# Seven-product Q/K projection: two products and the loads around them reordered, results stored over three products

## The chip, the cores and the metric

One core of a Trainium2 chip runs the whole kernel. The metric is the device time of one execution in microseconds (us); the median of a few runs is what counts.

## The reference

```python
x = A_x                                  # 1 x 2048 x 1024, float32
xn = _layernorm(x)
q, k, v = split_heads(xn @ wqkv)         # 32 heads of 32 columns
o = softmax(q k^T / sqrt(32)) v          # per head, over all 2048 positions
s = merge_heads(o) @ wo
g = silu(mish(xn @ w1 + b1) @ w2)        # inner width 3584
out = x + s * g
```

All inputs and the output are float32.

## The kernel before

Every large matrix product is done in float32r with both operands split: `high` is the value copied into float32r by ScalarE (`copy`), `low` is what is left (`low`, a subtraction on VectorE or GpSimd). A product is then three matmuls, high·high, high·low and low·high (`THREE`).

The kernel runs in stages. First x is normalised, transposed and split into eight resident tiles `xc[c][g]` (chunk c of 512 tokens, half g of the 1024 columns), while V is computed. Then comes the Q/K stage, which the change concerns. Last comes a long stage of attention and the two dense layers, whose order a planner writes out (`Plan`), and a short tail for the output product.

**The Q/K stage.** There are 16 rounds q. A round takes 128 columns of the Q part of `wqkv` (`raw` tile r0) and 128 of the K part (r1), each 1024 x 128, and two chunks of tokens: chunks 2 and 3 for q below 8, chunks 0 and 1 from q = 8. It makes the 2 x 2 blocks of the result with seven products in place of eight. The products of a round are numbered i = 0 to 6 and named `A11, S2, A12, S3, S1, A22, S4`; a product (q, i) is 12 matmuls of 128 x 512. Its two operands are
- a piece of W (`piece`): a quarter of r0 or r1, or a sum S1 to S4 of quarters that GpSimd makes (`w_sum`, line 551) one round ahead; ScalarE and VectorE split it (`wq` tiles, two of two pieces each);
- a half chunk of x, or a sum of such half chunks, in `X[0]` (q below 8) or `X[1]` (from 8). The sums T0 to T3 for the second half of the rounds lie in DRAM (`ts`); they are loaded 128 x 512 at a time into `traw` buffers by `t_load`, and split into x tiles whose last reader in the first half is past: T1 into xc[2][0], T2 into xc[2][1], T0 into xc[3][0], T3 into xc[1][0]. The odd one of each pair of quarters has its low part made by GpSimd. One plain x half chunk, `X[1][6]`, is read back from `xs` in four loads into xc[1][1] (`B_COUNT`).

Products of a round add up in three PSUM banks, x, y and z. What is finished is added to an earlier result by VectorE (`plus`, line 775), split by `out_` into a `qst` tile and stored to `qs` or `ks` by a DMA of ScalarE's queue.

**What sets the order.** The order is written by hand in one loop over `SEQ`. For product number n the loop emits the 12 matmuls; then, at even n, the pieces n + 2 and n + 3 with the loads and sums that hang on them; then what `later.at(t, ...)` had put off to this product (`later.tick`); from (11, 2) on two score matmuls of head 0 with a maximum on VectorE each (`s_mm`, lines 695 and 699); then `after()`, the copies and additions for the result; and last the loads counted from product (7, 0) by `since`. Each engine and queue then runs its own list in that order and waits where an operand or a buffer is not ready. SyncE's queue carries all loads.

`EARLY` moves a few products of rounds 7 and 8 forward, so that the x tiles come free for T0 to T3 before they are needed. `q_load` loads the two W tiles of a round (512 KB each) into the buffers of the round two before.

Of the kernel before, what the change touches and what calls it, by code (L numbers as in the profile page):

```python
# [9 lines left out]
F32 = mybir.dt.float32  # L10
# [8 lines left out]
P = 128  # L19
# [211 lines left out]
def body(ctx: ExitStack, tc: tile.TileContext, x, wqkv, wo, w1, b1, w2, out):  # L231
    nc = tc.nc
# [6 lines left out]
    def pool(stack, name, bufs, side="left", **kw):  # L239
        return stack.enter_context(tc.tile_pool(name=name, bufs=bufs, side=side, reuse_waits="tile", **kw))  # L240

    def psum(stack, name, bufs):
        return stack.enter_context(tc.tile_pool(name=name, bufs=bufs, space=PSUM, reuse_waits="tile"))
# [43 lines left out]
    def copy(out_, in_, scale=1.0):  # L287
        nc.scalar.activation(out_, in_, AF.Copy, scale=scale)  # L288

    def move(out_, in_, eng=None):  # L290

        (eng or nc.sync).dma_start(out_.bitcast(F32), in_.bitcast(F32))

    def low(eng, out_, in_, high):

        eng.tensor_tensor(out_, in_, high.bitcast(F32), ALU.subtract)  # L296
# [6 lines left out]
    later = Later()  # L303
# [231 lines left out]
    A11, S2, A12, S3, S1, A22, S4 = range(7)  # L535
    NQ = 2 * KT
    raws, sums, pieces = {}, {}, {}

    def q_load(q, tiles):
        raws[q] = tiles  # L540
        for half in range(2):
            col = half * D + q % KT * P
            nc.sync.dma_start(tiles[half], wqkv[:, col:col + P].rearrange("(k p) f -> p k f", p=P))

    def w_sum(eng, q, which, out_):
        (r0, r1), done = raws[q], sums.setdefault(q, {})
        done[which] = out_
        a, b, how = {S1: lambda: (r1[:, :HK], r1[:, HK:], ALU.add), S2: lambda: (done[S1], r0[:, :HK], ALU.subtract),
                     S3: lambda: (r0[:, :HK], r1[:, :HK], ALU.subtract),
                     S4: lambda: (r0[:, HK:], done[S2], ALU.subtract)}[which]()  # L550
        eng.tensor_tensor(out_, a, b, how)

    EARLY = {(6, 2): [(7, 0)], (6, 3): [(7, 2)], (6, 4): [(7, 1)], (7, 4): [(8, 0)]}
    MOVED = [x for v in EARLY.values() for x in v]
    SEQ = [x for q in range(NQ) for i in range(7) if (q, i) not in MOVED for x in [(q, i)] + EARLY.get((q, i), [])]
    held = {w: big.tile([P, HK, P], F32, tag=f"ws{w}", name=f"ws{w}") for w in (S1, S3, S4)}

    def piece(n, eng):
        q, i = SEQ[n]
        if n % 2 == 0:  # L560
            pieces["tile"] = w1_tile(f"wq{n // 2}")
        w = pieces[n] = pieces["tile"][:, :, n % 2 * HK:n % 2 * HK + HK]
        if i == A22:
            src = raws[q][1][:, HK:] if q else held[S3]
        else:
            src = raws[q][0][:, :HK] if i == A11 else raws[q][0][:, HK:] if i == A12 else sums[q][i]
        copy(w[:, 0], src, scale=-1.0 if i == A22 else 1.0)
        if i == A22:
            nc.vector.scalar_tensor_tensor(w[:, 1], src, -1.0, w[:, 0].bitcast(F32), op0=ALU.mult, op1=ALU.subtract)
        else:  # L570
            low(eng, w[:, 1], src, w[:, 0])
# [49 lines left out]
    halves = [(p, k, half) for p in (1, 0) for k in range(HK) for half in range(2)]  # L621
# [30 lines left out]
    ring = [ra.tile([P, KT, P], F32, name=f"raw{i}") for i in range(4)]  # L652
    qb = ExitStack()
    sp = pool(qb, "sp", 1)
    psq = psum(qb, "psq", 2)
    qst, kst = [], []

# [81 lines left out]
            move(dst[:, :, k], src[:, :, k])  # L739

    def t_load(i, k):
        raw, dst = sp.tile([P, 512], F32, tag="traw", name=f"t{i}_{k}", bufs=4), X[1][T_UNIT[i]]
        nc.sync.dma_start(raw, ts[i][:, k])

        def split():
            copy(dst[:, 0, k], raw)
            low(nc.gpsimd if k % 2 else nc.vector, dst[:, 1, k], raw, dst[:, 0, k])

        later.at(2, split)

    X = ([xc[2][0], xc[3][0], xc[2][1], xc[1][0], xc[1][1], xr, xc[3][1]],
         [xc[0][0], xc[2][0], xc[0][1], xc[2][1], xc[3][0], xc[1][0], xc[1][1]])
    BANK = ("x", "y", "x", "y", "z", "y", "z")
    T_UNIT = (4, 1, 3, 5)
    T_ORDER = [(i, k) for i in (1, 2, 0, 3) for k in range(HK)]
    T_COUNT = (2, 1, 1) * 4
    B_COUNT = {9: (0,), 10: (1,), 11: (2,), 12: (3,)}
    spare = []

    def ring_of(q):  # L760
        if q < KT + 2:
            return ring[q % 2 * 2:q % 2 * 2 + 2]
        if not spare:
            spare.append(big.tile([P, 4, KT, P], F32, tag="xc3_1", name="spare"))
        return [spare[0][:, q % 2 * 2 + half] for half in range(2)]

    def out_(q, half, chunk_, src):
        st = sp.tile([P, 2, 512], F32R, tag="qst", name=f"qst{q}_{half}_{chunk_}", bufs=4)
        copy(st[:, 0], src)
        low(nc.vector, st[:, 1], src, st[:, 0])  # L770
        dst = (qs, ks)[half][q % KT].rearrange("h p n -> p h n")[:, :, chunk_ * 512:(chunk_ + 1) * 512]
        later.at(2, lambda: move(dst, st, nc.scalar))

    def plus(out_, a, b):
        nc.vector.tensor_tensor(out_, a, b, ALU.add)
# [39 lines left out]
    for n, (q, i) in enumerate(SEQ):  # L815
        after = product(n)
        for m in (n + 2, n + 3) if n >= 2 and n % 2 == 0 else ():
            if m >= 7 * NQ:
                continue
            piece(m, nc.vector if q < 11 or m % 2 else nc.gpsimd)  # L820
            q_, i_ = SEQ[m]
            if i_ == A22:
                if q_ == 9:
                    ra_.close()
                    early = pool(att0, "early", 1, side="right")
                    stacks(early, 0)
                    stacks(early, 1)
                    hl_ = early.tile([P, P], F32R, name="hl")
                    nc.gpsimd.memset(hl_.bitcast(F32), 0.0)
                    nc.gpsimd.memset(early.tile([P, 32], F32, name="pad2"), 0.0)  # L830
                if q_ + 2 < NQ and q_ != 7:
                    q_load(q_ + 2, ring_of(q_ + 2))
            if q_ + 1 < NQ:
                for which in {S1: (S1, S2), A22: (S3,), S4: (S4,)}.get(i_, ()):
                    w_sum(nc.gpsimd, q_ + 1, which, s_tile(which))
        later.tick()
        if (q, i) >= (11, 2):
            for qt, kc in [x for _, x in zip(range(2), first_s)]:
                s_mm(0, qt, kc)
        after()  # L840
        since = n - SEQ.index((KT - 1, 0))
        if 0 <= since < len(T_COUNT):
            for _ in range(T_COUNT[since]):
                t_load(*T_ORDER.pop(0))
        if since == 11:
            q_load(9, ring_of(9))
        for k in B_COUNT.get(since, ()):
            move(X[1][6][:, :, k], xs[1][:, :, HK + k])
        if i == 0 and q == 10:
            load_head(0)  # L850
        if i == 3 and q == 14:
            load_head(1)
        if i == 5 and q == NQ - 1:
            load_w1(0)
# [638 lines left out]
    for c in range(NC):  # L1493
        for s in range(4):
            t = 4 * c + s
            if t + 4 < NT:
                start(t + 4)
            for dh in range(2):
                k = 2 * s + dh
# [45 lines left out]
```

## Time and profile before

| | |
|---|---|
| median of 3 runs | 3377.38 us (3376.79 to 3378.0) |
| the profiled execution | 3378.28 us |
| its span | 3376.5 us |
| TensorE busy | 3346.0 us, 99% of the span |
| VectorE, ScalarE, GpSimd busy | 74%, 61%, 75% |
| the Q/K stage | 202.16 us to 536.38 us of the span |

The span runs from the first instruction to the last; 1.78 us of the profiled execution lie outside it. Matmuls are pipelined: a product of 12 shows 2.88 us, while the next one starts 2.72 us after it. So the start-to-start distance is what tells whether TensorE was held up.

### The profile page before, as it was taken

To read this page: it belongs to the slowest core of one execution; us is meant where nothing else is said; L and a number is where in the kernel's file an instruction comes from. 1 tells how busy PE (TensorE), PEld (TensorE's weight loads), DVE (VectorE), ACT (ScalarE), POOL (GpSimd) and SP (SyncE) were. 2 spreads that over 40 slices of the span, in tenths; PEclk is the share of its full clock that TensorE was granted. 3 is DMA by queue.
4 is the path that set the end of the run, shared out by engine and by line. 5 is a ranking of instruction groups with operands and counts; after the bars stand their busy time and mean duration, and the time that the engine had idled before them with its cause. 6 is when DMAs were issued, how large, how long until landed. Compare 5 with 4: busy or idle time off the path is not lost.

```text
span 3376.5 us, 45751 instructions
## 1 busy us (share of the span) xinstructions
PE 3346.0 (99%) x16867; PEld 2455.0 (73%) x16867; DVE 2511.8 (74%) x3984; ACT 2055.8 (61%) x3314; POOL 2525.0 (75%) x751
## 2 busy tenths in 40 slices
PE   8999999999999999999999999999999999999999
PEld 7888777777777677777667767677667777767787
DVE  6665678888777777887888778788777888886542
ACT  5233425677667666667666766667667766667621
POOL 2322445999999977889888988888888898889800
PEclk9999999999999999999999999999999999999999
DMA  7864745455555643434344434333344433433482
GB/s 243 298 208 158 244 156 164 135 175 169 169 173 173 218 132 112 123 102 118 118 120 147 144 101 125 90 111 113 113 150 127 127 98 112 125 118 106 136 301 87
DMA packets 291460, 501.56 MB, mean 149 GB/s; under 512 B 88138, under 2 KB 151114, under 8 KB 269130
## 3 DMA queue, kind: packets, MB, share of 16 engines
q1 hardware_dynamic: 271524, 456.95, 43.8%
q10 hardware_dynamic: 19712, 41.69, 3.3%
q8 instruction: 133, 2.18, 0.3%
q14 instruction: 91, 0.75, 0.1%
HBM read 352.55 MB, written 144.97 MB: 147 GB/s over the span
## 4 chain that ended last, share of the span: by engine, by line
PE 93%; DMA 2%; DVE 2%; POOL 1%; issue 1%; ACT 1%; SPq 0%; ACTq 0%; DVEq 0%; POOLq 0%
PE y L1287 17%; PE h L1197 17%; PE t L992 13%; PE s L910 13%; PE pv L1039 13%; PE op L1386 5%; PE v L354 5%; PE q_y L790 3%; PE q_x L790 2%; PE q_z L790 2%; PE zp L1065 1%; POOL z L1021 1%; PE pt L423 0%; DVE mx L699 0%; DMA raw<-in_A_wqkv_dram 0%
## 5 line engine op out<-in xcount | busy, mean ns | idle before, releaser
L1021 POOL TENSOR_TENSOR z<-z,p 128x2048 f32<-128x2048 f32 x448 | 2068.3, 4617 | 98.2 <-ACT p L285 73.0
L285 ACT ACTIVATE p<-t,zero 128x512 f32<-128x512 f32 x2048 | 1376.6, 690 | 560.3 <-PE t L992 534.4
L916 DVE TENSOR_REDUCE mx<-s 128x1 f32<-128x512 f32 x1984 | 1321.8, 685 | 384.8 <-PE s L910 373.9
L1287 PE MATMUL y<-w,act 128*128 128x512 f32 x2688 | 920.5, 391 | 1.1 <-DVE yacc L1309 0.5
L992 PE MATMUL t<-qstack,kstack 128*128 128x512 f32 x2048 | 798.9, 393 | 2.9 <-DMA qstack<-mt 1.9
L910 PE MATMUL s<-kstack,qstack 128*128 128x512 f32 x1984 | 772.7, 393 | 0.9 <-ACT p L285 0.9
L1197 PE MATMUL h<-xr,w 128*128 128x512 f32 x2016 | 697.7, 391 | 0.5 <-DMA xr<-xs 0.5
L1287 PEld LDWEIGHTS y<-w,act 128*128 128x128 f32 x2688 | 503.2, 188 | 115.0 <-issue 6.7
L992 PEld LDWEIGHTS t<-qstack,kstack 128*128 128x128 f32 x2048 | 383.8, 188 | 117.2 <-issue 19.5
L1039 PE MATMUL pv<-p,v 128*32 128x512 f32 x4096 | 459.4, 594 | 0.0
L910 PEld LDWEIGHTS s<-kstack,qstack 128*128 128x128 f32 x1984 | 369.7, 188 | 119.2 <-issue 32.1
L1197 PEld LDWEIGHTS h<-xr,w 128*128 128x128 f32 x2016 | 378.3, 188 | 81.3 <-issue 3.4
L1309 DVE TENSOR_TENSOR yacc<-yacc,y 128x512 f32<-128x512 f32 x416 | 282.6, 680 | 82.5 <-PE y L1287 81.5
L1039 PEld LDWEIGHTS pv<-p,v 128*32 128x32 f32 x4096 | 123.3, 110 | 282.8 <-issue 281.4
L1021 POOL TENSOR_TENSOR z<-p,p 128x2048 f32<-128x2048 f32 x32 | 148.1, 4628 | 185.1 <-PE zp L1065 146.8
L1197 PE MATMUL h<-xc,w 128*128 128x512 f32 x672 | 231.2, 391 | 0.3 <-ACT p L285 0.3
L354 PE MATMUL v<-vw,xc 128*128 128x512 f32 x768 | 180.9, 394 | 0.8 <-DVE vw L296 0.7
L354 PEld LDWEIGHTS v<-vw,xc 128*128 128x128 f32 x768 | 143.5, 189 | 32.0 <-DVE vw L296 1.8
L1197 PEld LDWEIGHTS h<-xc,w 128*128 128x128 f32 x672 | 125.9, 188 | 29.0 <-issue 2.5
L790 PE MATMUL q_y<-xc,wq 128*128 128x512 f32 x480 | 116.2, 391 | 5.6 <-POOL xc L296 4.8
L288 ACT ACTIVATE act<-h 128x512 fp32r<-128x512 f32 x112 | 66.7, 595 | 87.7 <-DVE h L1246 86.4
L790 PEld LDWEIGHTS q_y<-xc,wq 128*128 128x128 f32 x480 | 90.1, 188 | 25.0 <-POOL xc L296 5.2
(146 smaller groups left out, 2940.8 us busy)
## 6 DMA issues: line engine op xcount, KB each, us to landing
w<-w1s SPq DMA_DIRECT2D x91, 1024.0 KB
w<-w2s SPq DMA_DIRECT2D x168, 512.0 KB
w2s<-w SPq DMA_DIRECT2D x56, 512.0 KB
qstack<-qs SPq DMA_DIRECT2D x96, 256.0 KB
kstack<-ks SPq DMA_DIRECT2D x96, 256.0 KB
w1s<-w SPq DMA_DIRECT2D x21, 1024.0 KB
qs<-qst ACTq DMA_DIRECT2D x32, 512.0 KB
ks<-qst ACTq DMA_DIRECT2D x32, 512.0 KB
```

Source lines behind the costliest of these rows:

```text
L285: nc.scalar.activation(out_, in_, fn, bias=zero if bias is None else bias, scale=scale)
L354: nc.tensor.matmul(ps, xc[t // 4][k // HK][:, a, k % HK, (t % 4) * P:(t % 4 + 1) * P], vw[i, k // 2][:, b, k % 2], start=n == 0, stop=n == ...
L790: nc.tensor.matmul(ps, w[:, a, k], xx[:, b, k], start=m == 0 and i in (0, 1, 4), stop=m == 3 * HK - 1, skip_group_check=i not in (0, 1, 4))
L910: nc.tensor.matmul(sp_, qst[h % 3][:, qt * P:(qt + 1) * P], kst[h % 3][:, kc * 512:(kc + 1) * 512], start=True, stop=True)
L916: nc.vector.reduce_max(tiles["mx"][:, qt, kc:kc + 1], tiles[qt, kc], axis=AX.X)
L992: nc.tensor.matmul(tp, kst[h % 3][:, kt * P:(kt + 1) * P], qst[h % 3][:, c * 512:(c + 1) * 512], start=True, stop=True)
L1021: nc.gpsimd.tensor_tensor(zs[h], pts[T - 1] if kt == 1 else zs[h], pts[T], ALU.add)
L1039: nc.tensor.matmul(pv[h][c * DH:(c + 1) * DH, :], vt[h][:, k, :], pts[T - kt + k][:, c * 512:(c + 1) * 512], start=k == 0, stop=k == NT - 1)
L1197: nc.tensor.matmul(t["h"], w1t[n][:, a, k], xts_[c][k // HK][:, b, k % HK], start=i == 0, stop=i == 3 * KT - 1)
L1287: nc.tensor.matmul(t["y"], acts[n][:, p, s * P:(s + 1) * P], w2t[m_][:, q], start=j == 0 and i == 0, stop=j == YB - 1 and i == 2)
L1309: nc.vector.tensor_tensor(ya, ya, t["y"], ALU.add)
L1386: nc.tensor.matmul(ps[t, dh], ohl[t // 4, k][:, a, s * P:(s + 1) * P], wt[k][:, b, r], start=k == 0 and i == 0, stop=k == KT - 1 and i == 2)
```

## The change

- `EARLY`: (7, 0) stands behind (6, 0), before it stood behind (6, 2); (7, 2) stands behind (6, 2), before behind (6, 3). Since `since` counts from (7, 0), the loads of T0 to T3 and of round 9's W come two products sooner.
- `t_load`: the `traw` buffers go to a pool of their own with five in place of four, and are split three products after the load in place of two.
- `B_COUNT`: the four loads of `X[1][6]` are asked for 12 to 15 products after (7, 0) in place of 9 to 12, which is one product later in all.
- `q_load` can load one half: r0 of round q + 2 is loaded when piece A12 of round q is made, r1 when piece A22 is; before, both at A22. Round 9's two tiles come at `since` 9 and 11, before both at 11.
- `out_`: ScalarE's copy comes one product after `after()`, VectorE's subtraction two after it and the store three after it; before, the first two were part of `after()` and the store came two after it.

```diff
-    def q_load(q, tiles):
+    def q_load(q, tiles, halves=range(2)):
         raws[q] = tiles
-        for half in range(2):
+        for half in halves:
...
-    EARLY = {(6, 2): [(7, 0)], (6, 3): [(7, 2)], (6, 4): [(7, 1)], (7, 4): [(8, 0)]}
+    EARLY = {(6, 0): [(7, 0)], (6, 2): [(7, 2)], (6, 4): [(7, 1)], (7, 4): [(8, 0)]}
...
+    tr_ = ExitStack()
+    tr = pool(tr_, "tr", 1)
...
-        raw, dst = sp.tile([P, 512], F32, tag="traw", name=f"t{i}_{k}", bufs=4), X[1][T_UNIT[i]]
+        raw, dst = tr.tile([P, 512], F32, tag="traw", name=f"t{i}_{k}", bufs=5), X[1][T_UNIT[i]]
...
-        later.at(2, split)
+        later.at(3, split)
...
-    B_COUNT = {9: (0,), 10: (1,), 11: (2,), 12: (3,)}
+    B_COUNT = {12: (0,), 13: (1,), 14: (2,), 15: (3,)}
...
-        copy(st[:, 0], src)
-        low(nc.vector, st[:, 1], src, st[:, 0])
         dst = (qs, ks)[half][q % KT].rearrange("h p n -> p h n")[:, :, chunk_ * 512:(chunk_ + 1) * 512]
-        later.at(2, lambda: move(dst, st, nc.scalar))
+        later.at(1, lambda: copy(st[:, 0], src))
+        later.at(2, lambda: low(nc.vector, st[:, 1], src, st[:, 0]))
+        later.at(3, lambda: move(dst, st, nc.scalar))
...
                 if q_ == 9:
                     ra_.close()
+                    tr_.close()
...
-                if q_ + 2 < NQ and q_ != 7:
-                    q_load(q_ + 2, ring_of(q_ + 2))
+            if i_ in ((A12, A22) if q_ else (A22,)) and q_ + 2 < NQ and q_ != 7:
+                q_load(q_ + 2, ring_of(q_ + 2), (i_ == A22,) if q_ else range(2))
...
-        if since == 11:
-            q_load(9, ring_of(9))
+        if since in (9, 11):
+            q_load(9, ring_of(9), (since == 11,))
```

**SyncE's queue around product (6, 0) to (6, 4).** `raw0` and `raw1` are the two W tiles of round 8, `t1_0` to `t2_3` the first eight loads of T1 and T2. Before:

```order
L543 DMA raw3_1898<-in_A_wqkv_dram 128x8x128
L743 DMA t1_0_2813<-ts1_137 128x512
L743 DMA t1_1_2815<-ts1_137 128x512
L743 DMA t1_2_2841<-ts1_137 128x512
L743 DMA t1_3_2862<-ts1_137 128x512
L543 DMA raw0_1895<-in_A_wqkv_dram 128x8x128
L543 DMA raw1_1896<-in_A_wqkv_dram 128x8x128
L743 DMA t2_0_2894<-ts2_138 128x512
```

The same place of the changed kernel:

```order
L543 DMA raw3_1898<-in_A_wqkv_dram 128x8x128
L543 DMA raw0_1895<-in_A_wqkv_dram 128x8x128
L745 DMA t1_0_2781<-ts1_137 128x512
L745 DMA t1_1_2783<-ts1_137 128x512
L745 DMA t1_2_2806<-ts1_137 128x512
L745 DMA t1_3_2821<-ts1_137 128x512
L745 DMA t2_0_2850<-ts2_138 128x512
L745 DMA t2_1_2852<-ts2_138 128x512
L745 DMA t2_2_2872<-ts2_138 128x512
L543 DMA raw1_1896<-in_A_wqkv_dram 128x8x128
L745 DMA t2_3_2903<-ts2_138 128x512
```

Four loads of T stood ahead of `raw1`, now seven do, and `raw0` has gone ahead of them all.

**GpSimd around product (8, 2).** `xc1_0` is the tile of T3, whose quarters 1 and 3 have their low part made here; `ws4`, `ws1`, `ws3` and `ws6` are the sums S1, S2, S3 and S4 of round 9's W. Before:

```order
L296 TENSOR_TENSOR xc1_0_185<-t3_1_3048,xc1_0_185 128x512
L551 TENSOR_TENSOR ws4_3137<-raw3_1898 128x512
L551 TENSOR_TENSOR ws1_3139<-ws4_3137,raw2_1897 128x512
L551 TENSOR_TENSOR ws3_3146<-raw2_1897,raw3_1898 128x512
L296 TENSOR_TENSOR xc1_0_185<-t3_3_3098,xc1_0_185 128x512
L551 TENSOR_TENSOR ws6_3184<-raw2_1897,ws1_3139 128x512
```

The same place of the changed kernel:

```order
L296 TENSOR_TENSOR xc1_0_185<-t3_1_3007,xc1_0_185 128x512
L296 TENSOR_TENSOR xc1_0_185<-t3_3_3057,xc1_0_185 128x512
L551 TENSOR_TENSOR ws4_3141<-raw3_1898 128x512
L551 TENSOR_TENSOR ws1_3143<-ws4_3141,raw2_1897 128x512
L551 TENSOR_TENSOR ws3_3148<-raw2_1897,raw3_1898 128x512
L551 TENSOR_TENSOR ws6_3186<-raw2_1897,ws1_3143 128x512
```

The last low part of T3 has gone ahead of three sums of round 9.

**ScalarE around products (11, 5) to (12, 0).** `qst11_1_0` and `qst11_0_1` are the copies of the results of (11, 5) and (11, 6), `wq43` the two pieces for (12, 2) and (12, 3). Before:

```order
L288 ACTIVATE qst11_1_0_3674<-q11_y_3548 128x512
L292 DMA ks3_73<-qst11_1_1_3647 128x2x512
L288 ACTIVATE qst11_0_1_3697<-q11_z_3626 128x512
L288 ACTIVATE wq43_3713<-spare_3143 128x512
L288 ACTIVATE wq43_3713<-ws3_3612 128x512
```

The same place of the changed kernel:

```order
L288 ACTIVATE qst11_1_0_3677<-q11_y_3551 128x512
L288 ACTIVATE wq43_3713<-spare_3095 128x512
L288 ACTIVATE wq43_3713<-ws3_3614 128x512
L292 DMA ks3_73<-qst11_1_1_3650 128x2x512
L288 ACTIVATE qst11_0_1_3699<-q11_z_3629 128x512
```

The copy of (11, 6)'s result stood ahead of the two pieces and now stands behind them. All instruction counts are the same; the lists differ only in the Q/K stage.

## The prediction

> **What bounds the kernel now.** First the page's busy times:
>
> ```profile
> PE 3346.0 (99%) x16867; PEld 2455.0 (73%) x16867; DVE 2511.8 (74%) x3984; ACT 2055.8 (61%) x3314; POOL 2525.0 (75%) x751
> ```
>
> TensorE is busy in 3346.0 of 3376.5 us. The change adds and removes no instruction, so it can only win time in which TensorE waits, or make it wait anew, and only in the Q/K stage, where the orders differ. Two stretches of that stage show such time in the table of busy times by stretch (length, then TensorE's busy time; PEclk is the granted clock):
>
> ```profile
> 349.00:384.00 35.00, 27.67 (x111) 21.60 (x111) 22.10 (x34) 16.00 (x29) 14.73 (x10) 0.95 0.86 278
> 430.00:537.00 107.00, 104.74 (x455) 84.45 (x454) 83.74 (x131) 30.38 (x59) 35.37 (x27) 1.00 0.44 142
> ```
>
> The first is the passage from rounds 7 to 8, the second the rounds with score matmuls. TensorE's timeline of the passage (start, length, instruction, in brackets the wait):
>
> ```profile
> 346.32 2.88 PE L790 MATMUL q_z<-xc,wq 128*128 128x512 f32 x12
> 350.84 3.40 PE L790 MATMUL q_x<-xc,wq 128*128 128x512 f32 x12 [1.64 <-ACT wq L288]
> ...
> 362.24 2.88 PE L790 MATMUL q_x<-xc,wq 128*128 128x512 f32 x12
> 365.94 3.00 PE L790 MATMUL q_y<-xc,wq 128*128 128x512 f32 x12 [0.81 <-DVE e L775]
> 368.78 2.88 PE L790 MATMUL q_z<-xc,wq 128*128 128x512 f32 x12
> 371.50 2.43 PE L790 MATMUL q_y<-xc,wq 128*128 128x512 f32 x10
> 378.73 1.14 PE L790 MATMUL q_y<-xc,wq 128*128 128x512 f32 x2 [4.81 <-POOL xc L296]
> 379.68 4.13 PE L790 MATMUL q_z<-xc,wq 128*128 128x512 f32 x12
> 383.64 2.89 PE L790 MATMUL q_x<-xc,wq 128*128 128x512 f32 x12
> ```
>
> A product that waits for nothing starts 2.72 us after the one ahead (368.78 to 371.50). From 346.32, product (7, 4), to 383.64, product (9, 0), are ten products, 27.20 us at that pace; they took 37.32. So 10.12 us are lost: 1.10 at (8, 3) (368.78 − 362.24 − 5.44), 6.70 at (8, 5) and the product behind it (383.64 − 371.50 − 5.44), and the other 2.32 at (8, 0), whose wait shows 1.64 and whose matmuls then ran 3.40 in place of 2.88. The term of 6.70 holds 1.24 us by which (8, 6) ran slow (383.64 − 379.68 − 2.72).
>
> That slowness is the granted clock, 0.95 in this stretch. The Trainium skill ("TensorE: Matmul & The Clock Gate", Part 1) says that a window of some 3.4 us idle halves the clock until a window of 3.4 us is busy. By that rule the slow part would cost an estimated 1.7 us and not 1.24, and the whole loss would come to 10.6 us.
>
> **Why TensorE waits there.** The last wait, for GpSimd. Its timeline, and from the chain of waits the transfer ahead of it:
>
> ```profile
> 373.09 1.81 POOL L551 TENSOR_TENSOR ws<-raw 128x512 f32<-128x512 f32 x1 [9.38 <-DMA raw<-in_A_wqkv_dram]
> ...
> 377.42 1.26 POOL L296 TENSOR_TENSOR xc<-t,xc 128x512 fp32r<-128x512 f32 x1
> ```
>
> ```profile
> 360.93 12.03 DMA raw<-in_A_wqkv_dram
> ```
>
> The low part of T3's last quarter (377.42) stands behind three sums of round 9, the first of which waits until 372.96 for W. And W was late because SyncE's queue was:
>
> ```profile
> 319.31 18.48 SPq L543 DMA_DIRECT2D raw<-in_A_wqkv_dram  x2
> 337.88 17.52 SPq L743 DMA_DIRECT2D t<-ts  x10
> ...
> 359.97 0.43 SPq L743 DMA_DIRECT2D t<-ts  x1
> 360.45 1.69 SPq L543 DMA_DIRECT2D raw<-in_A_wqkv_dram  x2
> 362.24 5.50 SPq L292 DMA_DIRECT2D xc<-xs  x2
> ```
>
> The second half of round 8's W holds the queue to 337.79, until its buffer's last piece is split; twelve of sixteen T loads follow it. The other two waits come from the same lateness. ScalarE makes the pieces of (8, 0) behind a result copy that waited:
>
> ```profile
> 349.67 0.60 ACT L288 ACTIVATE qst<-q_z 128x512 fp32r<-128x512 f32 x1 [2.25 <-DMA t<-ts]
> 350.17 1.14 ACT L288 ACTIVATE wq<-raw 128x512 fp32r<-128x512 f32 x2
> ```
>
> and at (8, 3) VectorE reaches the addition that frees the bank y late, behind a T split and a result's low part:
>
> ```profile
> 364.50 0.69 DVE L296 TENSOR_TENSOR xc<-t,xc 128x512 fp32r<-128x512 f32 x1
> 365.11 0.68 DVE L775 TENSOR_TENSOR e<-q_y,e 128x512 f32<-128x512 f32 x1
> ```
>
> **Part one: loads and sums of the passage.** With (7, 0) right behind (6, 0), all T loads are asked for two products, 5.44 us, sooner, and seven instead of four ahead of the load that blocks. Ahead of them now stands the first half of round 8's W; it goes out near 319.3, as the row of 319.31 shows, and T1's splits, at (7, 2), are not due before 327.3 (346.32 − 7 x 2.72). The second half, the load that blocks, stays near 337.4, since it waits for the same split. Behind it the ring of five `traw` buffers sets the pace, each load waiting for a split three products back. Working forward from 337.8 at 2.72 us a product, I estimate that T0's loads go out between 341 and 345, T3's between 346 and 351; before, T3's last went out at 359.97. A load took 5.12 us in the chain:
>
> ```profile
> 337.88 5.12 DMA t<-ts
> ```
>
> T3 then lies in SBUF by about 356, its splits stand at (8, 1) at the latest, 357.20 if nothing waits, and (8, 5) would start at 368.08: some 8 us to spare. GpSimd has the last low part ahead of the three sums, so their wait for W no longer holds TensorE. W's first half goes out near 348, the second near 351, where the pair went at 360.45; even at 12.03 us it lands by 363, ahead of the sums' use in round 9. So the 6.70 us go.
>
> With T there in time and result copies put off by a product, ScalarE comes to the pieces of (8, 0) without standing behind a copy that waits for VectorE: 2.32 us go. The addition before (8, 3) has no late split ahead of it on VectorE, as T3's last is GpSimd's and T3's third stands a product earlier: 1.10 us go.
>
> What is next: the loads of `X[1][6]`. The last three and round 10's W pass SyncE only after product (7, 6), at 357.2 undisturbed, because a half of that W takes the tile that (7, 6) reads, and stands ahead of them. These are 2.5 MB, and two stores of 0.5 MB beside them. The DMA engines in that time before:
>
> ```profile
> 357.00:373.00 16.00, 15.19 (x67) 12.26 (x66) 12.02 (x18) 8.65 (x16) 4.47 (x3) 1.00 1.02 328
> ```
>
> Full, at 328 GB/s (last column). At that rate 3.5 MB take 10.7 us, to 368; (8, 6) starts at 370.80 and reads the last quarter 2 us later. Hidden with 5 us to spare; uncovered, each us late costs one.
>
> What it can cost: splits of T now stand in VectorE's list ahead of the pieces for (6, 5), where before one less did. The first of those pieces, and what the splits take:
>
> ```profile
> 336.20 1.18 DVE L569 SCALAR_TENSOR_TENSOR wq<-raw,wq 128x512 fp32r<-128x512 f32 x1
> ```
>
> ```profile
> L296 DVE TENSOR_TENSOR xc<-t,xc 128x512 fp32r<-128x512 f32 x8 | 9.4, 1180 | 1.4 <-ACT xc L288 1.4
> L296 DVE TENSOR_TENSOR wq<-raw,wq 128x512 fp32r<-128x512 f32 x18 | 13.3, 744 | 1.9 <-ACT wq L288 1.9
> ```
>
> The piece was ready at 337.38 and (6, 5) starts at 338.16 (346.32 − 3 x 2.72): 0.78 us to spare. One more T split takes 1180 ns in the mean (744 for the same subtraction on W), so it costs 0 to 1.2 us; I take 0.5, near 1.18 − 0.78 = 0.40. The Trainium skill ("SBUF — State Buffer", its passage on the shared port pair) says that VectorE with two SBUF inputs and GpSimd lock each other out for a whole instruction. That speaks against splits beside GpSimd's sums; the 1180 ns agree, and by the rule the cost would be a whole GpSimd sum, an estimated 1.3 us, in place of 0.5.
>
> **Part two: results over three products.** In the score rounds TensorE and VectorE show this at (12, 1):
>
> ```profile
> 446.46 2.88 PE L790 MATMUL q_y<-xc,wq 128*128 128x512 f32 x12
> 450.33 1.09 PE L695 MATMUL s<-kstack,qstack 128*128 128x512 f32 x2 [0.99 <-DVE mx L699]
> 451.27 2.89 PE L790 MATMUL q_x<-xc,wq 128*128 128x512 f32 x12
> ```
>
> ```profile
> 447.28 0.69 DVE L296 TENSOR_TENSOR qst<-q_z,qst 128x512 fp32r<-128x512 f32 x1 [0.67 <-ACT qst L288]
> 448.32 1.36 DVE L296 TENSOR_TENSOR wq<-ws,wq 128x512 fp32r<-128x512 f32 x1 [0.35 <-ACT wq L288]
> 449.60 2.56 DVE L699 TENSOR_REDUCE mx<-s 128x1 f32<-128x512 f32 x4
> ```
>
> From 446.46 to 451.27 is 4.81 us, where 2.72 and a pair of score matmuls, 0.46, would do: 1.63 lost. VectorE waited for ScalarE's copy of (11, 6)'s result and then for the pieces behind that copy, 1.02 us in sum, and the maxima came late. TensorE waited so twice:
>
> ```profile
> PE s L695 <- DVE mx L699: 2.0, 2, 1.0
> ```
>
> so 3.3 us in all. In the new order ScalarE makes the pieces first, and VectorE's subtraction stands a product behind the copy. Both idle times go and with them the wait: 3.3 us. The store is later by one product; nobody reads it for several rounds, and the four `qst` buffers keep their distance, since the copy into the next one is a product later as well. PSUM banks come free a product or two later, but are asked for again two rounds on. Halves of W loaded apart cost nothing, as the first is asked for earlier and the second where it was. These edits I cost at nothing.
>
> **The sum.** Against the profiled execution: 3378.28 − 10.1 − 3.3 + 0.5 = 3365.4. That execution lies 0.9 us over the median of the runs, 3377.38, so the time is 3364.5 us. A measurement of this kernel tells about 0.2%, 6.75 us, from no change: below 3370.6 is faster.
>
> **The rivals.**
> 1. *The score waits stay*: VectorE is busy in 83.74 of 107 us there, and its delay may come from the two pieces of one product alone. Then 3377.4 − 10.1 + 0.5 = 3367.8. Against it: the 1.02 us of idle time stand right ahead of the maxima. Chance 0.12.
> 2. *A new wait at (8, 6)*: SyncE's queue held by W for round 10, full DMA engines, `X[1][6]` late. For it speaks the share of 1.02 above, and the 5.50 us for which SyncE was held at 362.24. If it costs what the wait at (8, 5) did, 6.70 us, the time is 3371.2; at half of that, 3367.9. Chance 0.14, split evenly at 3370.6. The Trainium skill ("Trainium Kernel Development and Optimization", Key Constraints) says that loads of all issuing engines share the same 16 DMA engines; by that, asking sooner adds no bandwidth, which is this rival's case.
> 3. *No gain*: TensorE's lost time only moves inside the stage, 3377 us. Against it: T and W go out 9 us sooner. Chance 0.04.
> 4. *Slower*: put off, the low parts of results pile up on VectorE ahead of the maxima. In the score rounds, every second of 32 products has its pieces split there; if each such product stalled as the two do now, 16 x 1.63 − 13.4 = +12.7 us, 3390. It decides from 13 such products on (21.2 us, 7.8 over the gain). For it: VectorE's 78% load in that stretch; against it: the waits on ScalarE that leave it. Chance 0.10.
>
> **The numbers.** The forecast, 3364.5, has 0.60. Low end: the 0.5 isn't paid, and the rounds with scores give back all that they lose; of their 107 us, 32 products with their pairs need 32 x 3.18 = 101.8, so up to 1.9 us go beyond the 3.3: 3362.1, and 0.6 for the spread of the runs gives 3361.5. High end: rival 2 at its full price, 3371.5. Outside lie rivals 3 and 4, 0.14. Faster: 0.60 + 0.12 + half of rival 2 and a little of the bounds, 0.80; same 0.10; slower 0.10.
>
> **What would show it.** Right: TensorE's timeline from 316 to 384 shows products 2.72 us apart throughout, round 9 starts near 373.5, the granted clock of the passage is 1.0, T3's last load goes out near 350, GpSimd has its low part ahead of the sums, and no score matmul waits 1 us for a maximum. Wrong: a wait of more than 1 us at (6, 5) or (8, 6), score waits at more than a few products, or a stage that is shorter while the span is not.

## The result and the profile after

| | before | changed |
|---|---|---|
| median of 15 runs | 3376.72 us (3375.53 to 3378.28) | 3370.50 us (3368.13 to 3374.08) |
| the profiled execution, its span | 3378.28, 3376.5 us | 3371.32, 3369.5 us |
| first matmul of the last stage | 536.38 us | 530.75 us |
| time lost from (7, 4) to (9, 2) | 10.12 us | 8.78 us |
| time lost in the 32 products with scores (rounds 11 to 15) | 4.96 us | 0.44 us |

The ratio is 0.9982, 95% interval 0.9975 to 0.9988: 6.2 us sooner, in the range given and half of the 12.9 us forecast. "Lost" is, here and below, each product's start-to-start distance over 2.72 us (with a score pair, 3.173, which is 14 matmuls at the same pace), added up from TensorE's timeline. The gain is not where most of it was expected: the passage gave 1.34 us of its 10, the score rounds 4.52.

The page's busy times, then the two stretches that the prediction read (length, busy times of TensorE, its weight loads, VectorE, ScalarE, GpSimd; granted clock; DMA share; GB/s):

```profile
PE 3344.0 (99%) x16867; PEld 2455.6 (73%) x16867; DVE 2510.7 (75%) x3984; ACT 2056.4 (61%) x3314; POOL 2526.6 (75%) x751
```

```profile
349.00:384.00 35.00, 29.83 (x119) 23.40 (x119) 24.72 (x32) 14.36 (x26) 14.83 (x10) 0.91 0.82 270
430.00:537.00 107.00, 106.63 (x472) 87.84 (x471) 84.28 (x138) 33.00 (x64) 34.49 (x26) 1.00 0.49 155
```

The second stretch is now full: TensorE is busy in 106.63 of 107 us, before in 104.74. The first is still not, and its granted clock is 0.91, where it was 0.95 before. TensorE's timeline of the changed kernel says where:

```profile
349.29 2.88 PE L792 MATMUL q_x<-xc,wq 128*128 128x512 f32 x12
353.58 3.00 PE L792 MATMUL q_y<-xr,wq 128*128 128x512 f32 x12 [1.41 <-DVE e L777]
...
365.34 2.98 PE L792 MATMUL q_y<-xc,wq 128*128 128x512 f32 x12 [0.50 <-DVE e L777]
...
370.88 2.88 PE L792 MATMUL q_y<-xc,wq 128*128 128x512 f32 x12
373.60 2.20 PE L792 MATMUL q_z<-xc,wq 128*128 128x512 f32 x9
379.06 1.65 PE L792 MATMUL q_z<-xc,wq 128*128 128x512 f32 x3 [3.26 <-DMA xc<-xs]
380.50 4.89 PE L792 MATMUL q_x<-xc,wq 128*128 128x512 f32 x12
385.23 2.91 PE L792 MATMUL q_y<-xc,wq 128*128 128x512 f32 x12
```

(8, 5), which before lost 6.70 us together with the product behind it, runs through at 370.88. The product behind it, (8, 6), stops after nine matmuls for the last load of `X[1][6]`: 4.18 us lost there and 2.01 at (9, 0), which runs at a lower clock. With 1.57 at (7, 5), 0.76 at (8, 3) and 0.26 elsewhere that makes 8.78.

The chain of waits shows what (8, 6) waited for, and SyncE's queue why it came late (start, how long the issue held the queue, load, how many):

```profile
355.09 9.26 DMA raw<-in_A_wqkv_dram
364.37 14.64 DMA xc<-xs
```

```profile
337.82 14.76 SPq L745 DMA_DIRECT2D t<-ts  x7
...
353.15 1.89 SPq L745 DMA_DIRECT2D t<-ts  x2
355.09 0.88 SPq L543 DMA_DIRECT2D raw<-in_A_wqkv_dram  x1
356.06 3.21 SPq L292 DMA_DIRECT2D xc<-xs  x1
360.32 0.39 SPq L543 DMA_DIRECT2D spare<-in_A_wqkv_dram  x1
360.77 2.89 SPq L292 DMA_DIRECT2D xc<-xs  x2
363.70 0.60 SPq L543 DMA_DIRECT2D spare<-in_A_wqkv_dram  x1
364.37 5.32 SPq L292 DMA_DIRECT2D xc<-xs  x1
```

The last of the four loads of `X[1][6]` stands behind both halves of round 10's W (`spare`); its issue alone takes 5.32 us, and it lands at 379.01. This is rival 2 of the prediction.

In the score rounds, the place of (12, 1):

```profile
445.10 2.88 PE L792 MATMUL q_y<-xc,wq 128*128 128x512 f32 x12
447.82 0.62 PE L697 MATMUL s<-kstack,qstack 128*128 128x512 f32 x2
448.27 2.88 PE L792 MATMUL q_x<-xc,wq 128*128 128x512 f32 x12
```

3.17 us from product to product, where it was 4.81. VectorE has the maxima done in time; TensorE waits for none.

### The profile page after: what moved, and what is told of

Read it like the earlier page. It is cut to its first block, busy times and chain, and to the rows that moved or that the text cites. A ratio compares the mean times of both kernels' runs of the same rounds, so it can differ in the third digit from the quotient of the medians.

```text
span 3369.5 us, 45748 instructions
## 1 busy us (share of the span) xinstructions
PE 3344.0 (99%) x16867; PEld 2455.6 (73%) x16867; DVE 2510.7 (75%) x3984; ACT 2056.4 (61%) x3314; POOL 2526.6 (75%) x751
## 4 chain that ended last, share of the span: by engine, by line
PE 87%; DMA 2%; DVE 1%; ACT 0%; issue 0%; SPq 0%; ACTq 0%; POOL 0%; DVEq 0%
PE y L1290 18%; PE h L1200 18%; PE t L995 14%; PE s L913 13%; PE pv L1042 13%; PE op L1389 5%; PE q_y L792 2%; PE q_x L792 1%; PE q_z L792 1%; PE zp L1068 1%; PE s L697 0%; DMA xc<-xs 0%; DMA raw<-in_A_wqkv_dram 0%; DMA qstack<-mt 0%; DMA w2r<-in_B_w_dram 0%
```

## The experiments

Medians are of 6 to 11 runs, each with the ratio to the kernel before on the same chip; four kernels have a single run. What is said of the passage and the score rounds comes from the profile of one run of each kernel, and that run need not be the median one: for `old_results` it took 3370.15 us (median 3372.36), for `mixed` 3371.03 (median 3368.01). The medians tell of the whole.

**1. The new treatment of results alone.** `results_only` is the kernel before with the new `out_` and nothing else of the change:

```diff
-        copy(st[:, 0], src)
-        low(nc.vector, st[:, 1], src, st[:, 0])
-        later.at(2, lambda: move(dst, st, nc.scalar))
+        later.at(1, lambda: copy(st[:, 0], src))
+        later.at(2, lambda: low(nc.vector, st[:, 1], src, st[:, 0]))
+        later.at(3, lambda: move(dst, st, nc.scalar))
```

> The kernel before with the new treatment of results alone (copy, subtraction and store one, two and three products later). Both theories: no score matmul waits 1 us for a maximum; from the first score matmul to the end of the stage about 102 us in place of 106.5. Theory A (with the subtraction late, the store on ScalarE's queue waits for VectorE and holds ScalarE, and with it the splits of T): the passage, from product (7, 4) to (9, 0), loses at least the 10.1 us of before, and the time is 3372 to 3376 us. Theory B (the results' delay relieves ScalarE in the passage too): it loses less than 8 us there, and the time is 3368 to 3371.

3374.22 us, ratio 0.9989 (0.9981 to 0.9998). The score rounds lose 0.46 us, so this edit alone does the whole of part two. The passage loses 8.03, between the two expectations: 2.1 us less than before, since (8, 0), whose pieces ScalarE makes, now starts 2.72 us after (7, 4), while the wait for GpSimd stays (4.25 us).

**2. The change without it.** `old_results` is the changed kernel with the old `out_`, the diff above backwards.

> The changed kernel with the results treated as before (copy and subtraction in the same product, store two later). Both theories: the two score waits of 1 us are back, score rounds about 106.5 us. Theory A (late stores hold ScalarE in the passage): T goes out sooner, the passage loses under 6 us in place of 8.8, and the time is 3370 to 3372, about that of the changed kernel. Theory B (the passage is bound by the loads of X[1][6] behind W of round 10 and full DMA engines): the passage loses 8 to 10 us as in the changed kernel, and the time is 3374 to 3376.

3372.36 us, ratio 0.9985 (0.9976 to 0.9994). The score loss is back at 4.94 us, and the passage loses only 3.18, as theory A had it: the reordered loads win 6.9 of the 10.1 us that part one promised, as long as results are treated the old way. The wait at (8, 6) is gone. In this kernel SyncE's last load of `X[1][6]` reads:

```profile
361.58 2.84 SPq L292 DMA_DIRECT2D xc<-xs  x1
```

It goes out 2.8 us sooner, in a passage that itself begins 0.9 us sooner, and holds the queue half as long; it still stands behind both halves of W. So inside the change the two parts hurt each other: by these profiles the new `out_` gains 4.5 us in the score rounds and costs 8.78 − 3.18 = 5.6 in the passage. The whole times do not tell the two kernels apart: their ratios, 0.9982 and 0.9985, lie well within each other's intervals. Why shows in the busy times of 345 to 357, of the changed kernel and then of `old_results`:

```profile
345.00:357.00 12.00, 10.59 (x47) 8.47 (x46) 10.48 (x13) 6.58 (x13) 6.93 (x6) 1.00 0.55 151
```

```profile
345.00:357.00 12.00, 10.86 (x47) 8.29 (x46) 9.64 (x12) 7.24 (x15) 6.51 (x6) 1.00 0.77 241
```

and in what SyncE's DMA queue (q1, the loads) and ScalarE's (q10, the stores) carried in that time (packets, MB, share), in the same order:

```profile
q1 hardware_dynamic: 1057, 1.25, 43.0%
q10 hardware_dynamic: 288, 0.56, 12.1%
```

```profile
q1 hardware_dynamic: 1762, 1.84, 53.4%
q10 hardware_dynamic: 544, 1.05, 23.5%
```

The DMA engines stand at 0.55 just ahead of the crowd, 0.77 with the old results: half a megabyte of stores and 0.6 of loads have moved out of this time. In the next 16 us, when `X[1][6]` and W are asked for, the stores of the changed kernel take

```profile
q10 hardware_dynamic: 1292, 2.50, 41.0%
```

2.50 MB, against 1.80 in `old_results`. And a store holds ScalarE itself: its subtraction is now so near ahead that ScalarE, in order, waits for it. ScalarE's and VectorE's timelines of the changed kernel:

```profile
345.86 0.37 ACTq L292 DMA_DIRECT2D ks<-qst  x1
346.27 0.63 ACT L288 ACTIVATE xc<-t 128x512 fp32r<-128x512 f32 x1 [4.01 <-issue]
```

```profile
344.01 1.77 DVE L296 TENSOR_TENSOR qst<-e,qst 128x512 fp32r<-128x512 f32 x1
```

The store of `ks` leaves at 345.86, when the low part started at 344.01 is done (345.78); ScalarE stood idle 4.01 us up to then, and the T split behind the store, with the buffer that it frees, waited too.

**3. The store a product later.** `store4` takes that hold away and leaves the rest of the new order:

```diff
-        later.at(3, lambda: move(dst, st, nc.scalar))
+        later.at(4, lambda: move(dst, st, nc.scalar))
```

> The changed kernel with the store of a result four products after it in place of three, so that ScalarE comes to it a product after the subtraction. Theory A: the idle time of ScalarE of 4.0 and 3.4 us ahead of T's copies at 346 and 353 us goes, T3's last load goes out before 352 in place of 355, X[1][6]'s last load lands 3 us sooner, the passage loses under 5 us, 3365 to 3367 us. Theory B: ScalarE waits less but the last load lands as late as now, the passage loses 8 to 9 us, 3369 to 3372 us.

3369.89 us, ratio 0.9978 (0.9969 to 0.9987); the passage loses 5.64 us, between the two expectations. The T split behind that store now waits 2.65 us for its load and no longer for the store, but T3's last load is out at 355.0, as in the changed kernel, and not before 352. The wait at (8, 6) is shorter but there:

```profile
377.88 1.48 PE L792 MATMUL q_z<-xc,wq 128*128 128x512 f32 x3 [2.11 <-DMA xc<-xs]
379.16 4.01 PE L792 MATMUL q_x<-xc,wq 128*128 128x512 f32 x12
```

So the place of the store is a part of it. That the order of the loads is the rest is what the next run asks.

**4. `X[1][6]` ahead of round 10's W.** `x_first` is the changed kernel with the four loads asked for before SyncE comes to that W:

```diff
-    B_COUNT = {12: (0,), 13: (1,), 14: (2,), 15: (3,)}
+    B_COUNT = {11: (0, 1), 12: (2, 3)}
```

> The changed kernel with the four loads of X[1][6] asked for at 11 and 12 products after (7, 0), ahead of both halves of round 10's W. If the order behind that W is what makes (8, 6) wait: the wait of 3.3 us and the slow clock behind it go, 6.2 us in all; the passage loses about 2.6 us, 3364 to 3366 us. If the DMA engines are merely full, the loads of T3 or round 9's W are pushed back instead and another product waits: the passage loses over 6 us, 3368 to 3371 us.

3366.59 us (3365.73 to 3368.19), ratio 0.9968 (0.9956 to 0.9980). The passage loses 2.57 us: what was expected if the queue's order is the cause; the time is 0.6 us above the expected range. SyncE's queue, then TensorE at (8, 5), (8, 6) and (9, 0):

```profile
356.16 5.83 SPq L292 DMA_DIRECT2D xc<-xs  x4
362.78 10.75 SPq L543 DMA_DIRECT2D spare<-in_A_wqkv_dram  x3
```

```profile
370.88 2.88 PE L792 MATMUL q_y<-xc,wq 128*128 128x512 f32 x12
373.60 2.88 PE L792 MATMUL q_z<-xc,wq 128*128 128x512 f32 x12
376.32 2.88 PE L792 MATMUL q_x<-xc,wq 128*128 128x512 f32 x12
```

All four loads are out by 361.99 in place of 369.69; W takes the waiting (10.75 us in the queue), and nobody misses it. The DMA engines are as full as before this edit (share 1.07 from 357 to 373, 1.08 in the changed kernel), so with this much traffic it is the order that decides. The order alone does not make the wait: in `old_results` the same load stands behind both halves of W and comes in time, with 1.80 MB of stores in these 16 us in place of 2.50. The wait at (8, 6) and the slow product behind it, 6.2 us, are gone; what is left is 1.56 at (7, 5), 0.76 at (8, 3) and 0.25 elsewhere.

**5 and 6. Old results in the passage, new ones after it.** `mixed` is the changed kernel with the old treatment for rounds below 9, where no scores are computed yet; `mixed_x` has the edit of `x_first` as well.

```diff
+        if q < 9:
+            copy(st[:, 0], src)
+            low(nc.vector, st[:, 1], src, st[:, 0])
+            later.at(2, lambda: move(dst, st, nc.scalar))
+            return
```

> The changed kernel with results treated as before up to round 8 and in the new way from round 9 on. If the late subtraction and store hurt only in the passage and help only in the score rounds, the two add: the passage loses about 3.2 us as with old results, the score rounds about 0.5 us over 32 products as in the changed kernel; 11 us under the kernel before, 3366 to 3367 us. If the score rounds' gain needs the state in which the passage left the queues, the score waits come back or the passage loses 8 us, and the time stays at 3370 to 3372.

> As mixed, and the four loads of X[1][6] ahead of round 10's W. If that order matters only because the changed kernel comes late to it: the passage loses 2.5 to 3.2 us, the same as mixed within 1 us, 3365 to 3367 us. If early loads of X[1][6] push back something else where the DMA engines are less late: the passage loses over 4 us, 3367 to 3369 us.

`mixed`: 3368.01 us, ratio 0.9972 (0.9960 to 0.9983), passage 3.83, scores 0.47. `mixed_x`: 3367.6 us, ratio 0.9973 (0.9962 to 0.9983), passage 3.06, scores 0.46. Both times lie 0.6 to 1 us above the ranges given for the two effects adding up. With old results in the passage the order of the loads is worth 0.8 us, with new ones 6.2: each edit cures the same wait (`mixed` keeps 0.47 us of it), and both together are no better than `x_first` alone.

**7. W tiles whole again.** `whole_w` undoes the halves:

```diff
-            if i_ in ((A12, A22) if q_ else (A22,)) and q_ + 2 < NQ and q_ != 7:
-                q_load(q_ + 2, ring_of(q_ + 2), (i_ == A22,) if q_ else range(2))
+            if i_ == A22 and q_ + 2 < NQ and q_ != 7:
+                q_load(q_ + 2, ring_of(q_ + 2))
...
-        if since in (9, 11):
-            q_load(9, ring_of(9), (since == 11,))
+        if since == 11:
+            q_load(9, ring_of(9))
```

> The changed kernel with both halves of every W tile loaded together where piece A22 is made, round 9's at 11 products after (7, 0). Theory A (a half of round 10's W ahead of X[1][6] makes (8, 6) wait): X[1][6]'s loads now stand ahead of it, the wait at (8, 6) goes, the passage loses 2.5 to 5 us. Theory B (halves are needed, since W of round 9 comes late without them): a product waits for round 9's sums or the passage loses 8 us and more.

One run, 3374.16 us, passage 8.03. The expectation of a short passage held all four loads of `X[1][6]` to be ahead of W then. The queue shows that the fourth was not:

```profile
359.01 5.59 SPq L292 DMA_DIRECT2D xc<-xs  x3
364.70 5.17 SPq L543 DMA_DIRECT2D spare<-in_A_wqkv_dram  x2
369.92 3.77 SPq L292 DMA_DIRECT2D xc<-xs  x1
```

Its issue ends at 373.69, and (8, 6) waited 2.16 us for it. That and the slow clock behind it make 3.9 of the 8.03 us; the other 4.1 are lost at (7, 5), which waits 2.15 us for an addition. The run can't tell what the halves are worth by themselves; it shows once more that the load behind W is the one waited for.

**8. The old places of (7, 0) and (7, 2).** `old_early` keeps all of the change but this:

```diff
-    EARLY = {(6, 0): [(7, 0)], (6, 2): [(7, 2)], (6, 4): [(7, 1)], (7, 4): [(8, 0)]}
+    EARLY = {(6, 2): [(7, 0)], (6, 3): [(7, 2)], (6, 4): [(7, 1)], (7, 4): [(8, 0)]}
```

> The changed kernel with the order of products of before, so that everything counted from (7, 0) comes two products later. Theory A (the loads' place in SyncE's queue sets when T arrives): T3's last load goes out after 358 us in place of 355, the wait at (8, 5) comes back, the passage loses 10 us or more. Theory B (the ring of buffers and the splits on ScalarE set T's pace): T3's last load goes out within 2 us of 355 and the passage loses 8 to 9 us as now.

One run, 3371.8 us. T3's last load is out at 361.6 (360.4 in the kernel before), and the old wait at (8, 5) is back:

```profile
PE q_y L792 <- POOL xc L296: 4.3, 1, 4.3
```

So the two moved products, with the loads that are counted from them, are what takes it away. The passage loses 6.30 us in all, less than expected, since nothing else in it waits: the losses at (7, 5) and (8, 3) are absent here. That is 2.5 us less than in the changed kernel: with the loads of `X[1][6]` behind W, moving the products exchanged a loss of 6.3 us at (8, 5) for one of 6.2 at (8, 6) and added those two.

**9. Four buffers and two products for T.** `four_raw`:

```diff
-        raw, dst = tr.tile([P, 512], F32, tag="traw", name=f"t{i}_{k}", bufs=5), X[1][T_UNIT[i]]
+        raw, dst = tr.tile([P, 512], F32, tag="traw", name=f"t{i}_{k}", bufs=4), X[1][T_UNIT[i]]
...
-        later.at(3, split)
+        later.at(2, split)
```

> The changed kernel with four buffers for T's loads and the split two products after the load, as before. Theory A (a split holds its buffer no longer than it must when ScalarE comes to it late anyway, so the fifth buffer only makes up for the third product): T3's last load goes out within 2 us of the changed kernel's 355, and the passage loses 7 to 10 us. Theory B (the fifth buffer carries the earlier loads): it goes out after 357, (8, 5) waits for T3 again, and the passage loses over 11 us.

One run, 3368.41 us, passage 3.77, outside both expectations. T came no later (the last load out at 354.55), there is no wait at (8, 6), and 2.9 us are lost at (8, 2) and (8, 3) to late pieces and additions. The fifth buffer isn't what brings T sooner. The last load of `X[1][6]` stands behind both halves of W here too and goes out at 364.64, but its issue takes 1.74 us in place of 5.32. As in `old_results`, fewer stores were left for 357 to 373 (1.76 MB), and (8, 6) came 1.8 us later; why the stores were through sooner stays open.

**10 and 11. Who makes the low parts of T.** Both start from `x_first`, to find its last 2.5 us: `t_pool` gives all low parts of T to GpSimd, `t_dve` all to VectorE.

```diff
-            low(nc.gpsimd if k % 2 else nc.vector, dst[:, 1, k], raw, dst[:, 0, k])
+            low(nc.gpsimd, dst[:, 1, k], raw, dst[:, 0, k])     # t_pool
+            low(nc.vector, dst[:, 1, k], raw, dst[:, 0, k])     # t_dve
```

> The changed kernel with X[1][6]'s loads ahead of round 10's W and all sixteen low parts of T on GpSimd. Theory L (the waits left at (7, 5) and (8, 3), 2.6 us, come from VectorE's list, lengthened by T's subtractions that stand against GpSimd's): with eight fewer on VectorE they go, the passage loses under 1.5 us, 3364 to 3366 us. Rival: GpSimd, with eight more of 1.5 us, makes W's sums or T late; the passage loses 2.6 us or more, 3366 to 3370 us.

> The same with all sixteen low parts of T on VectorE. Theory L: the waits at (7, 5) and (8, 3) grow, the passage loses over 4 us. Rival (it is the meeting with GpSimd's own T parts that lengthens VectorE's instructions): VectorE's subtractions for T take about 0.7 us and the passage loses under 2.6 us.

`t_pool`: 3366.82 us, ratio 0.9969 (0.9957 to 0.9981), passage 2.70. `t_dve`: one run, 3367.18 us, passage 2.12. The theory that the number of T splits on VectorE makes these waits falls: taking them off VectorE empties the wait at (7, 5), but (8, 3) then loses 1.59 and (8, 6) 0.66; with eight more, (7, 5) loses 0.91 in place of 1.56, (8, 3) 0.97 in place of 0.76, and the passage less than in `x_first`. Both of the rival's figures for `t_dve`, about 0.7 us for a split and under 2.6 for the passage, came. What the splits take (shortest, median, longest in ns), on VectorE in the changed kernel, on VectorE in `t_dve`, on GpSimd in `t_pool`:

```profile
L296 DVE TENSOR_TENSOR xc<-t,xc x8: 677/754/1773, 333.1 to 362.7; 128x512 fp32r<-128x512 f32 x8
```

```profile
L296 DVE TENSOR_TENSOR xc<-t,xc x16: 677/679/1810, 334.4 to 363.7; 128x512 fp32r<-128x512 f32 x16
```

```profile
L296 POOL TENSOR_TENSOR xc<-t,xc x16: 1271/1739/1822, 332.9 to 364.9; 128x512 fp32r<-128x512 f32 x16
```

A split alone takes 0.68 us on VectorE; beside a GpSimd instruction it takes up to 1.8. The more GpSimd does, the more of VectorE's other work is stretched: its subtractions for the pieces made from sums take 0.73 us in the mean in `t_dve`, 0.74 in `x_first` and 1.26 in `t_pool`, where GpSimd is busy for 9.7, 21.7 and 33.0 of the 34 us from 332 to 366. The additions, which read a PSUM bank, are not: in the changed kernel that of 345.70 took 0.68 us, all of it beside GpSimd's sum of 345.31. What is left at (7, 5) and (8, 3) stays open.

**12. The old distance of `X[1][6]`.** `old_x` is the changed kernel with `B_COUNT` as it was:

```diff
-    B_COUNT = {12: (0,), 13: (1,), 14: (2,), 15: (3,)}
+    B_COUNT = {9: (0,), 10: (1,), 11: (2,), 12: (3,)}
```

> The changed kernel with the four loads of X[1][6] counted as before, 9 to 12 products after (7, 0). If their place behind round 10's W is what lets (8, 6) wait: all four now stand ahead of it, the wait goes, the passage loses 2 to 4 us, 3366 to 3368 us. If instead their first one, which waits for (7, 4), holds T3's last two loads behind it on SyncE's queue: T3's last load goes out after 358 us, (8, 5) waits, the passage loses over 6 us, 3370 us or more.

3382.48 us, ratio 1.0015 (1.0006 to 1.0024). Counted from a (7, 0) that moved, the first load now stands ahead of product (7, 4), which still reads the old contents of that tile. In this kernel (7, 4) takes a quarter of `X[1][6]` in their place, so that part of the computation is changed, and it waits for the load:

```profile
361.29 4.91 PE L792 MATMUL q_z<-xc,wq 128*128 128x512 f32 x12 [14.69 <-DMA xc<-xs]
```

The run says nothing on the order of the loads, which was its question (`x_first` answers it). It shows that the new `B_COUNT` is not a free choice: the loads had to go later once (7, 0) went sooner, and that put them behind W.

## Why the prediction was right, and where it was not

**Sign and range held, the make-up did not.** Forecast 3364.5, measured 3370.5. The time lies in the range only because its upper end was set at the full price of rival 2; the main line failed at (8, 6), and the wait of more than 1 us there is one of the signs that the prediction named for being wrong. Part of the shortfall in the passage was made good by the score rounds, which gave more than their term.

*T comes sooner, the 6.70 us at (8, 5) go*: right in kind. GpSimd has T3's last low part ahead of the sums:

```profile
363.70 1.30 POOL L296 TENSOR_TENSOR xc<-t,xc 128x512 fp32r<-128x512 f32 x1 [2.06 <-ACT xc L288]
365.96 1.67 POOL L551 TENSOR_TENSOR ws<-raw 128x512 f32<-128x512 f32 x1 [0.95 <-DVE wq L296]
```

It is done at 365.0, and (8, 5) starts at 370.88 without a wait; run 8 shows that the moved products do it. Mis-sized: T3's last load was to go out by 351 and was out at 355.0, 8.5 us after the start of (7, 4) in place of 4.7. The pace of a split each 2.72 us did not hold. That ScalarE is held by stores is the smaller part of it: counted in the same way it is 8.2 us with the old results, 7.6 in `store4` and 7.4 in `four_raw`. The rest stays open.

*"Hidden with 5 us to spare" for `X[1][6]`*: this step failed, and 6.2 us with it. It let 3.5 MB go at 328 GB/s from 357.2. What moved from 357 to 373 was 6.0 MB (3.51 on SyncE's queue, 2.50 on ScalarE's), at

```profile
357.00:373.00 16.00, 15.50 (x69) 12.38 (x68) 13.41 (x18) 8.01 (x15) 11.78 (x8) 1.00 1.08 377
```

377 GB/s. The rate was better than taken, but the amount was far larger. The second half of round 9's W was still in flight (issued at 355.09, landed at 364.35), and five stores' worth of results moved where two had been counted. The row on which the step rested already spoke against 3.5 MB: 16 us at 328 GB/s are 5.2 MB. The second slip is in the same step: all of it was taken to start at 357.2, while the load that (8, 6) needs last, behind both halves of W, went out at 364.37. Rival 2 had the place, the mechanism and the price (6.70 at its full size, 6.2 measured, for a time of 3371.2), with a chance of 0.14: too low, since the DMA share of 1.02 in its favour was already in the rows. Its sentence from the Trainium skill ("Trainium Kernel Development and Optimization", Key Constraints), that all issuing engines share 16 DMA engines, fits this trace: in these 16 us the loads' queue took a share of 66.7% and the stores' queue 41.0%, 1.08 together.

*(8, 0) and (8, 3), 2.32 + 1.10*: half right. (8, 0) starts on time, at 349.29. But (7, 5) behind it loses 1.57 to an addition that stands behind a T split of 1.77 us, and (8, 3) keeps 0.76. Of 3.42 us, 1.1 were won.

*0.5 us at (6, 5)*: not paid; the products from (6, 0) to (7, 4) lose nothing. The price by the Trainium skill's rule on the shared port pair ("SBUF — State Buffer", section "SBUF: two separate sides"), an estimated 1.3 us, is not paid there either. A little later the rule agrees: VectorE's low part of 344.01 took 1.77 us, where most take 0.68, beside a sum that GpSimd began at 343.56 and that took 1.67.

*3.3 us of score waits*: the mechanism right as far as runs 1 and 2 show it (they switch the loss off and on with `out_` as a whole, 0.46 and 4.94, and do not tell its three delays apart), the term too small. It counted the two waits of 1 us; the other products lost another 1.7 us in pieces of 0.1 to 0.45, which no row of the waits shows, and most of that went too. Measured 4.52, inside the 1.9 us left open above the term. Rival 4, low parts piling up ahead of the maxima, did not come.

*Stores, PSUM and halves at nothing*: for the new place of the results wrong by 5.6 us in the passage (run 2; 5.0 by run 5). This is the same loss as the 6.2 at (8, 6) and not a further one: with `X[1][6]` ahead of W the new place costs nothing (2.57 us in run 4, 3.06 in run 6). The halves of W were not told apart from the order of the loads (run 7). The losses at (7, 5) and (8, 3) were as large with the old results (1.63, of which 0.75 shows as a wait for a piece, and 1.20), so the later release of the PSUM banks did not add to them. "Nobody reads it for several rounds" is true of the data; but the store occupies ScalarE's list, the `qst` buffer and the DMA engines, and those were wanted.

With `x_first` the passage comes out as forecast, but for the 2.3 us at (7, 5) and (8, 3): 3366.59 us, the best time of the kernels here; `t_pool`, `mixed` and `mixed_x` have intervals that overlap with it. The span fell by 7.0 us, and the Q/K stage ended 5.6 us sooner: the last stage took 2838.8 us, 1.4 less than before, with the same lists of instructions. Between all these kernels it varies from 2838.8 to 2843.2, so this part is put down to neither edit.

## What to carry to other kernels

When loads are pulled forward, write out the queue behind them, with what each issue waits for: the load that ends up last is the one to cost, by all the bytes in flight ahead of it, stores included, and not by its own size. An operation that nobody reads soon is not free: ask what its list, its buffer and the DMA engines do meanwhile. And when a counter's starting point moves, every distance counted from it moves too; here one had to be lengthened to stay right, and that put the urgent load behind one that could wait.

## What the runs showed that was not expected

What the slow clock costs after a wait does not grow with the wait. The granted clock of the changed kernel after its wait of 3.26 us, by windows of 2 us:

```profile
378.00:380.00 2.00, 0.94 (x2) 0.83 (x3) 0.00 (x0) 0.00 (x0) 0.00 (x0) 0.50 0.97 341
380.00:382.00 2.00, 2.00 (x6) 1.54 (x5) 1.26 (x2) 0.52 (x1) 0.00 (x0) 0.50 0.10 35
382.00:384.00 2.00, 2.00 (x6) 1.52 (x6) 0.03 (x1) 0.07 (x1) 0.00 (x0) 0.50 0.00 0
```

and of `store4` after its wait of 2.11 us:

```profile
378.00:380.00 2.00, 2.00 (x5) 1.52 (x6) 0.60 (x1) 0.00 (x0) 0.00 (x0) 0.53 0.68 252
```

Beyond the wait itself, the waiting product and the next one lost 1.9 us in `store4`; after the two waits of 2.15 and 2.16 us in `whole_w` it was 1.9 and 1.8, after 4.81 us in the kernel before 1.9, after 14.69 in `old_x` 2.0, and 2.9 in the changed kernel. In windows of 0.2 us the clock stands at 0.50 for the same length of time after most of these waits: from 378.84 to 382.26 in the kernel before and from 378.1 to 381.5 in `store4`, 3.4 us each. In the changed kernel it is twice that, 377.9 to 384.7, of which TensorE spent the first 1.2 us still waiting; half of the other 5.6 us is 2.8, close to the 2.9 lost. So a wait of 2.1 us costs some 4. A wait of 1.41 us, (7, 5) in the changed kernel, cost next to nothing beyond itself (0.16), and the clock stayed at 1.00; it did so after the 1.64 us at (8, 0) in the kernel before too. The Trainium skill ("TensorE: Matmul & The Clock Gate", Part 1) speaks of a window of some 3.4 us idle and one of 3.4 us busy. The second agrees with the 3.4 us above, and the estimated 1.7 us that the prediction worked out from it is near the 1.8 to 2.0 of most waits. The first does not agree: waits of 2.11 us were enough.
